# A planned fused kernel (complex linear attention and two MLPs): each kind of transfer, and the attention's matmuls, get a duration of their own in the planner

## The chip, the cores and the metric

The kernel runs on one core of a Trainium2 chip. The metric is device time in microseconds (us), lower is better. The profile is one execution of the whole program, taken by the hardware profiler; its times count from the start of its span.

## The reference, cut to what matters

Sizes: batch 4, 8 heads, 768 steps, head size 48; the MLPs are 384 wide with 2048 hidden units.

```python
scale = minimum(mag, 0.999) / (mag + 1e-6)        # mag = |a_re + i a_im|
for t in range(S):                                # complex decay, real k v, per head
    S_re, S_im = ar*S_re - ai*S_im + k_t v_t, ar*S_im + ai*S_re
    y[t] = q_t @ S_re
x = y as (4*768) rows of 384
h = x @ w_in1;  x = maximum(0.01*h, h) @ w_out1
h = x @ w_in2;  out = where(h > 0, h, exp(min(h, 0)) - 1) @ w_out2
```

## The kernel before

**Attention.** The recurrence is cut into chunks of 128 steps: 6 chunks times 4 batches give 24 tiles, `attention(0)` to `attention(23)`. ACT and DVE turn the decays of a tile into products of magnitudes and sums of angles. DVE writes scaled k and q into the tile `st` (L459, one product for the cosine half and one for the sine half). The two halves leave for a scratch in HBM (L466, `stack_scratch<-st`) and come back in another layout as `f` (L469, `f<-stack_scratch`): two transfers out, two transfers in. PE transposes `st` (L485), multiplies `f` by `f` into scores (L498), and DVE masks them into `am` (L503). PE multiplies scores and state by v (L513, or L536 and L541), and from tile 3 on the result goes through a second scratch (L550 out, L553 back as `y`) and is split into two halves of 16 bits, `xh` and `xl` (L347, L348). L569 (`kv`) and the DVE steps L578 and L581 bring the running state up to date. There is one buffer for `st` and one for `f`.

**MLPs.** A block is three tiles, 384 columns. Eight blocks pass the first MLP and eight the second, in the order of the list ORDER. Each block runs over 16 slices of the hidden units. For a slice, L598 is a group of 9 matmuls into `h` (weights and inputs are pairs of 16-bit halves, three products over three column groups); ACT and DVE make `g` of it and split it (L607 to L612, L347, L348); L633 is a group of 9 matmuls into `acc`. The weights arrive as 64-bit words in 64 pieces (`wr`, three buffers, L311 and L314), and five steps on DVE and ACT convert a piece (L333, L335, L338, L341, L342). At the end of the list ACT reads the decays and weights once more for checks of range.

**What sets the order.** Nothing runs where it is written. Each step is given to `plan.op` with its engine, a duration, and what it reads and writes. `schedule` is a list scheduler: it walks through time, starts on each engine the ready step of the best rank, and takes an engine as busy for the duration given. `order` runs it three times with ranks improved from a backward pass and keeps the plan that ends first. The instructions are then issued in the order of the planned starts, so each engine's queue is fixed before the chip sees it: an instruction that waits on the chip holds everything behind it on its engine. A transfer is two steps: the issue on SP (475 ns) and the transfer itself on one "DMA" engine of the plan, with 650 ns ahead of it and some 900 to 1070 ns behind. The duration of the transfer was its bytes over 360, in ns. Where the plan shows PE idle for over 700 ns, the gap is filled with small matmuls on a constant (L753, `h<-ident`), (gap - 300) / 220 of them, so that PE does not lose its clock.

```python
if eng == "SP":
    self.ops.append([eng, self.ISSUE, fn, deps, due])
    self.ops.append(["DMA", ns / self.RATE, None, {m}, due])     # RATE = 360.0
```

Of the kernel before, what the change touches and what calls it, by code (L numbers as in the profile page):

```python
# [21 lines left out]
B, H, S, D = 4, 8, 768, 48  # L22
P = 128
C = 128
NC = S // C
NT = NC * B
DM = H * D
# [1 line left out]
DFF = 2048  # L29
KF = DFF // P  # L30
CW = 2 * C + 1
TILE_BYTES = 4 * DM * C
LAG = 2
SIZES = [3] * 8
ORDER = [1, 1, 1, 2, 1, 2, 1, 2, 1, 2, 1, 2, 1, 2, 2, 2]
# [86 lines left out]
class Plan:  # L122
# [8 lines left out]
            ("DMA", "DVE"): 907.0, ("DMA", "ACT"): 908.0, ("DMA", "PE"): 1067.0, ("DMA", "POOL"): 983.0}  # L131
    SWITCH = 1300.0
    ISSUE = 475.0
    RATE = 360.0
    ROUNDS = 3
    LAST = 1e9

# [7 lines left out]
    def op(self, eng, ns, fn, r=(), w=(), table=None, due=None):  # L145
        if table is not None and table != self.table:
            self.table = table
            self.ops.append([eng, self.SWITCH, lambda: self.load(table), set(self.group), None])
            self.group = [len(self.ops) - 1]
        m = len(self.ops)  # L150
        n = m + 1 if eng == "SP" else m
        deps = set()
        for x in r:
            deps.update(x.writers)
        for x in w:
            deps.update(x.writers)
            deps.update(x.readers)
        for x in (*r, *w):
            root = x.root
            if root.before is not None and not x.writers:  # L160
                deps.update(root.before.users)
            if root.last is not None and not root.users:
                deps.update(root.last.users[:1])
            root.users.append(n)
        for x in r:
            x.readers.append(n)
        for x in w:
            x.writers.append(n)
        if table is not None:
            deps.add(self.group[0])  # L170
            self.group.append(n)
        deps.discard(n)
        due = self.due if due is None else due
        if eng == "SP":
            self.ops.append([eng, self.ISSUE, fn, deps, due])
            self.ops.append(["DMA", ns / self.RATE, None, {m}, due])
        else:
            self.ops.append([eng, ns, fn, deps, due])

# [52 lines left out]

EXTRA = 97.0
SCAN = 350.0
YNS = 130.0
WARM = 8000.0
WARM_GAP = 700.0

# [9 lines left out]
def tile_due(i):  # L248
    return None
# [11 lines left out]
def fast_path(ctx, tc, aa, kq, vt, w_in1, w_out1, w_in2, w_out2, st_dram, yt_dram, out):  # L261
    nc = tc.nc
# [20 lines left out]
    plan = Plan(lambda table: nc.scalar.preload_act_table_set(sets[table]))  # L283
# [21 lines left out]
    def load_w(which, part, k):  # L305
        src = w_src[which, part].bitcast(I32)
        raw = plan.buf(cp, [P, DM, 2], I32, "wr", WR_BUFS)

        def load():
            if part == "in":  # L310
                nc.sync.dma_start(raw.t.rearrange("p (j f) w -> p j (f w)", j=KJ),  # L311
                                  src[:, 2 * k * P:2 * (k + 1) * P].rearrange("(j p) f -> p j f", p=P))
            else:
                nc.sync.dma_start(raw.t.rearrange("p o w -> p (o w)"), src[k * P:(k + 1) * P, :])  # L314

        plan.op("SP", 2 * TILE_BYTES, load, w=[raw])
        return raw

    def check_w(which, part, k, raw):
# [48 lines left out]
    def check_later(i):  # L368
        c, b = divmod(i, B)
        ar, ai = plan.buf(cp, [P, KJ, C], F32, "re"), plan.buf(cp, [P, KJ, C], F32, "im", 2)  # L370
        m2, sq = plan.buf(cp, [P, KJ, C], F32, "t0"), plan.buf(cp, [P, KJ, C], F32, "t8")
        plan.op("SP", TILE_BYTES, lambda: nc.sync.dma_start(ar.t, aa[c, b, :, 0]), w=[ar])
        plan.op("SP", TILE_BYTES, lambda: nc.sync.dma_start(ai.t, aa[c, b, :, 1]), w=[ai])
        check_re(i, ar, sq)
        plan.op("ACT", act(DM), lambda: S_.activation(sq.t, ai.t, AF.Square), r=[ai], w=[sq])
        plan.op("ACT", act(DM), lambda: S_.activation(m2.t, ar.t, AF.Square), r=[ar], w=[m2])
        plan.op("DVE", dve(DM), lambda: V.tensor_tensor(m2.t, m2.t, sq.t, ALU.add), r=[sq], w=[m2])
        check_m2(i, m2, sq)

    def attention(i):  # L380
        c, b = divmod(i, B)
# [3 lines left out]

        N = KJ * C
        ar, ai = plan.buf(cp, [P, KJ, C], F32, "re"), plan.buf(cp, [P, KJ, C], F32, "im", 2)
        plan.op("SP", TILE_BYTES, lambda: nc.sync.dma_start(ar.t, aa[c, b, :, 0]), w=[ar])
        plan.op("SP", TILE_BYTES, lambda: nc.sync.dma_start(ai.t, aa[c, b, :, 1]), w=[ai])
        x = plan.buf(cp, [P, KJ, 2, C], F32, "kq", 3)  # L390
        re, im = (lambda: ar.t), (lambda: ai.t)
        m2, sq, yr, t = tmp(0), tmp(8), tmp(1), tmp(2)
# [13 lines left out]
        w = tmp(3)  # L406
# [7 lines left out]
        def scan_p():  # L414
# [11 lines left out]
        plan.op("DVE", dve(N), lambda: V.tensor_tensor(tp.t, pr.t[:, :, 1], yp.t, ALU.mult), r=[pr, yp], w=[tp])  # L426
        plan.op("DVE", dve(N), lambda: V.scalar_tensor_tensor(
            pr.t[:, :, 0], tp.t, 2.0, yp.t, ALU.subtract, ALU.mult, reverse0=True), r=[tp, yp], w=[pr])
        plan.op("SP", 2 * TILE_BYTES, lambda: nc.sync.dma_start(x.t, kq[c, b]), w=[x])
        plan.op("DVE", dve(2 * N), lambda: V.tensor_tensor(x.t, x.t, pr.t, ALU.mult), r=[pr], w=[x])  # L430
        yield
        th = tmp(7)
# [30 lines left out]
        scr = st_dram[i % 2]  # L463
        dr = plan.buf(None, None, None, "scr", 2)
        for cs in range(2):
            plan.op("SP", 4 * DM * CW, lambda cs=cs: nc.sync.dma_start(  # L466
                scr[cs].rearrange("(j p) w -> p j w", p=P), st.t[:, cs]),
                r=[st.part(("e", cs)), st.part(cs)], w=[dr.part(cs)])
            plan.op("SP", 4 * DM * CW, lambda cs=cs: nc.sync.dma_start(  # L469
                f.t[D * cs:D * (cs + 1)], scr[cs].rearrange("(h d) w -> d h w", d=D)), r=[dr.part(cs)],  # L470
                w=[f.part(cs)])
        fp = [f.part(0), f.part(1)]

        v = plan.buf(cp, [P, H, D], F32, "v")
        plan.op("SP", TILE_BYTES, lambda: nc.sync.dma_start(v.t, vt[c, b]), w=[v])
        last = c == NC - 1
        pa = lambda: plan.buf(ps_a, [P, 512], F32, "pa", 3)
        if not last:
# [13 lines left out]
        for g in range(2):  # L492
            pt = pa()

            def sc(g=g, pt=pt):
                for hh in range(4):
                    h = 4 * g + hh
                    T_.matmul(pt.t[:, hh * C:(hh + 1) * C], lhsT=f.t[:, h, 0:C], rhs=f.t[:, h, C:2 * C],  # L498
                              start=True, stop=True)

            plan.op("PE", 4 * 218, sc, r=fp, w=[pt], due=tile_due(i))
            m = plan.buf(cp, [P, 4, C], F32, "am", 2)
            plan.op("DVE", dve(512), lambda m=m, pt=pt: V.tensor_tensor(  # L503
                m.t, pt.t.rearrange("p (h t) -> p h t", h=4), mask.unsqueeze(1).to_broadcast([P, 4, C]), ALU.mult),
                r=[pt], w=[m])
            am.append(m)
# [20 lines left out]
        else:  # L527
# [19 lines left out]
                yt.t[:wide].rearrange("p g t -> p (g t)"), py.t[:wide], AF.Copy, scale=SX), r=[py], w=[yt])  # L547
            yd, ys = yt_dram[i % 2], plan.buf(None, None, None, "yscr", 2)
            for r in range(2):
                plan.op("SP", TILE_BYTES // 2, lambda r=r: nc.sync.dma_start(  # L550
                    yd.rearrange("(g r e) t -> r e g t", r=2, e=D)[r], yt.t[64 * r:64 * r + D]), r=[yt], w=[ys.part(r)])
            y = plan.buf(cp, [P, KJ, C], F32, "y")
            plan.op("SP", TILE_BYTES, lambda: nc.sync.dma_start(y.t, yd.rearrange("(j p) t -> p j t", p=P)),  # L553
                    r=[ys.part(0), ys.part(1)], w=[y])
            xsrc, xap = y, lambda: y.t
        k, q = place[i]
# [7 lines left out]
        if not last:  # L564
            pk = pa()

            def kv():
                for h in range(H):
                    T_.matmul(pk.t[:2 * D, h * D:(h + 1) * D], lhsT=kn.t[:, h].rearrange("p a d -> p (a d)"),  # L569
                              rhs=v.t[:, h, :], start=True, stop=True)  # L570

            plan.op("PE", 8 * 163, kv, r=[kn.part(0), kn.part(1), v], w=[pk], due=tile_due(i))
            pk3 = lambda: pk.t[:2 * D, :DM].rearrange("p (h e) -> p h e", h=H)
            pe = lambda: f.t[:, :, 2 * C:2 * C + 1].to_broadcast([2 * D, H, D])
            if c == 0:
                plan.op("ACT", act(N, True), lambda: S_.activation(state[b].t, pk3(), AF.Copy), r=[pk], w=[state[b]])
            else:
                plan.op("DVE", dve(N), lambda: V.tensor_tensor(state[b].t, pk3(), state[b].t, ALU.add),  # L578
                        r=[pk], w=[state[b]])
            if c % 2:  # L580
                plan.op("DVE", dve(N), lambda: V.tensor_tensor(state[b].t, state[b].t, pe(), ALU.mult),  # L581
                        r=fp, w=[state[b]])
# [34 lines left out]
    def block(which, k):  # L617
# [38 lines left out]
        for o in range(outs):  # L656
            c, b = divmod(blk[o], B)
            e = plan.buf(cp, [P, DM], F32, "o", 2)
            if o % 2:
                plan.op("DVE", dve(DM), lambda o=o, e=e: V.tensor_scalar(  # L660
                    e.t, acc[o].t[:, :DM], 1.0 / (SG * SW), None, ALU.mult), r=[acc[o]], w=[e])
            else:
                plan.op("ACT", act(DM, True), lambda o=o, e=e: S_.activation(
                    e.t, acc[o].t[:, :DM], AF.Copy, scale=1.0 / (SG * SW)), r=[acc[o]], w=[e])
            plan.op("SP", TILE_BYTES, lambda e=e, r0=b * S + c * C: nc.sync.dma_start(out[r0:r0 + C, :], e.t), r=[e])


    running = {i: attention(i) for i in range(NT)}
# [268 lines left out]
```

## Time and profile before

| | |
|---|---|
| runs | 1018.89, 1020.98, 1015.18 us; median 1018.89 |
| profiled execution, its own time | 1022.27 us |
| its span | 1020.6 us |
| PE busy (matmuls) | 942.7 us, 92% |
| PE weight loads | 628.7 us, 62% |
| ACT busy | 723.8 us, 71% |
| DVE busy | 688.3 us, 67% |
| POOL busy | 52.4 us, 5% |
| transfers of the SP queue | 127.97 MB, 45.2% of 16 engines' span |

PE is busy for nearly the whole span, but busy is not even over it: the first fifth holds most of its idle time, and there DVE, ACT and the transfers are dense too. From about 345 us to the end PE hardly stops. PE's clock is granted in full (2.4 GHz) or in half (1.2 GHz), and the half shows in short stretches behind idle ones. The matmuls on a constant count as busy PE.

### The profile page before, as it was taken

The numbers are of one execution on the slowest core, as the hardware profiler recorded it, in microseconds if no ns is written. First come the engines' busy times: TensorE is split into PE (matmuls) and PEld (weight loads), VectorE is DVE, ScalarE is ACT, GpSimd is POOL, SyncE is SP. The second block draws the span as 40 slices with busy tenths as digits, with TensorE's granted clock in tenths as the row PEclk, the third lists the DMA queues.
The fourth block names the chain that finished last, engine by engine and source line by source line (L and its number), as shares of the span: only waits on it lengthen the run. The fifth ranks groups of instructions, "written<-read, shape, count | busy, mean of one in ns | idle before, by whom it ended". The sixth has DMA issues, their size and how long they took to land.

```text
span 1020.6 us, 17938 instructions
## 1 busy us (share of the span) xinstructions
PE 942.7 (92%) x6486; PEld 628.7 (62%) x6486; DVE 688.3 (67%) x1450; ACT 723.8 (71%) x1686; POOL 52.4 (5%) x113
## 2 busy tenths in 40 slices
PE   4487988899999899999999989999999999999997
PEld 3486756556666665666666766575566666666664
DVE  7898887889998873685657777755644443544452
ACT  6576763668868763785568678899899998855552
POOL 4001300100000000000000000000000000000000
PEclk8699899999999999999999999999999999999999
DMA  6787966654556631440231565244746644000000
GB/s 227 197 226 190 254 145 169 168 155 115 157 170 182 182 80 39 122 127 17 70 94 55 138 158 162 85 111 147 210 155 167 191 153 135 32 1 24 2 24 27
DMA packets 110033, 129.20 MB, mean 127 GB/s; under 512 B 6768, under 2 KB 98672, under 8 KB 109936
## 3 DMA queue, kind: packets, MB, share of 16 engines
q1 hardware_dynamic: 109936, 127.97, 45.2%
q8 instruction: 53, 0.87, 0.4%
q14 instruction: 44, 0.36, 0.1%
HBM read 100.15 MB, written 27.80 MB: 125 GB/s over the span
## 4 chain that ended last, share of the span: by engine, by line
PE 59%; DMA 16%; ACT 11%; DVE 10%; issue 3%; POOL 1%; SPq 1%; ACTq 0%; DVEq 0%; POOLq 0%
PE acc L633 26%; PE h L598 25%; DMA f<-stack_scratch 6%; PE pa L498 3%; DMA stack_scratch<-st 3%; ACT t L324 2%; DMA turned_scratch<-am 2%; DMA y<-turned_scratch 2%; ACT gh L347 1%; PE pa L569 1%; PE pa L536 1%; DMA wr<-in_w_out 1%; DVE st L459 1%; ACT g L609 1%; PE pa L541 1%
## 5 line engine op out<-in xcount | busy, mean ns | idle before, releaser
L633 PE MATMUL acc<-gh,w1out 128*128 128x384 f16 x768 | 188.8, 328 | 4.0 <-DVE yl L650 2.4
L633 PE MATMUL acc<-w2out,gh 128*128 128x384 f16 x768 | 188.0, 327 | 0.2 <-DVE yl L650 0.2
L348 DVE TENSOR_TENSOR gl<-g,gh 128x384 f16<-128x384 f32 x256 | 141.2, 552 | 67.7 <-ACT gh L347 65.5
L612 DVE SCALAR_TENSOR_TENSOR g<-h,g 128x384 f32<-128x384 f32 x256 | 141.5, 553 | 54.7 <-ACT g L607 51.3
L347 ACT ACTIVATE gh<-g 128x384 f16<-128x384 f32 x256 | 132.5, 518 | 60.6 <-PE acc L633 56.4
L598 PEld LDWEIGHTS <-w1in 128*128 128x128 f16 x1152 | 113.6, 99 | 80.3 <-issue 8.5
L633 PEld LDWEIGHTS <-w1out 128*128 128x128 f16 x1152 | 113.0, 99 | 77.6 <-issue 7.5
L598 PEld LDWEIGHTS <-w2in 128*128 128x128 f16 x1152 | 112.3, 98 | 75.6 <-issue 2.7
L598 PE MATMUL h<-xh,w1in 128*128 128x384 f16 x768 | 148.2, 330 | 4.6 <-DVE g L612 4.4
L598 PE MATMUL h<-yh,w2in 128*128 128x384 f16 x768 | 145.8, 326 | 1.3 <-DVE g L612 1.3
L633 PE MATMUL acc<-gl,w1out 128*128 128x384 f16 x384 | 126.0, 328 | 0.0
L633 PE MATMUL acc<-w2out,gl 128*128 128x384 f16 x384 | 125.4, 326 | 0.0
L611 DVE TENSOR_SCALAR g<-g 128x384 f32<-128x384 f32 x128 | 45.7, 357 | 115.3 <-ACT g L610 115.1
L609 ACT ACTIVATE g<-h 128x384 f32<-128x384 f32 x128 | 62.1, 485 | 65.6 <-PE h L598 51.6
L633 PEld LDWEIGHTS <-gh 128*128 128x128 f16 x768 | 74.7, 98 | 48.6 <-issue 2.5
L607 ACT ACTIVATE g<-h 128x384 f32<-128x384 f32 x128 | 61.8, 483 | 49.6 <-PE h L598 31.7
L598 PE MATMUL h<-xl,w1in 128*128 128x384 f16 x384 | 84.4, 329 | 0.0
L598 PE MATMUL h<-yl,w2in 128*128 128x384 f16 x384 | 83.3, 326 | 0.0
L498 PE MATMUL pa<-f 96*128 96x128 f32 x384 | 56.4, 301 | 29.1 <-DMA f<-stack_scratch 25.6
L324 ACT ACTIVATE t<-wt,consts 128x384 f32<-128x384 f32 x128 | 78.0, 609 | 1.3
L498 PEld LDWEIGHTS pa<-f 96*128 96x128 f32 x384 | 52.7, 212 | 33.8 <-issue 23.5
L610 ACT ACTIVATE g<-g 128x384 f32<-128x384 f32 x128 | 66.5, 520 | 2.1
(111 smaller groups left out, 1259.4 us busy)
## 6 DMA issues: line engine op xcount, KB each, us to landing
wr<-in_w_in SPq DMA_DIRECT2D x64, 384.0 KB, 3.4
wr<-in_w_out SPq DMA_DIRECT2D x64, 384.0 KB, 3.4
stack_scratch<-st SPq DMA_DIRECT2D x48, 385.5 KB, 4.7
f<-stack_scratch SPq DMA_DIRECT2D x48, 385.5 KB, 5.8
kq<-in_kq SPq DMA_DIRECT2D x24, 384.0 KB, 5.0
re<-in_aa SPq DMA_DIRECT2D x32, 192.0 KB, 2.9
im<-in_aa SPq DMA_DIRECT2D x32, 192.0 KB, 3.0
v<-in_v SPq DMA_DIRECT2D x24, 192.0 KB, 3.1
```

What stands on the lines that cost most here:

```text
L324: plan.op("ACT", act(DM) + 2 * EXTRA, lambda side=side, scale=scale, bias=bias: S_.activation(z.t, t.t, AF.Relu, scale=scale, bias=bias, a ...
L347: plan.op("ACT", eng, lambda: S_.activation(hi(), v(), AF.Copy), r=r, w=wh)
L348: plan.op("DVE", dve(n), lambda: V.tensor_tensor(lo(), v(), hi(), ALU.subtract), r=r + wh, w=wl)
L459: plan.op("DVE", dve(2 * N), lambda cs=cs, tab=tab: V.tensor_tensor(st.t[:, cs, :, 0:2 * C].rearrange("p j (k t) -> p j k t", k=2), x.t, t ...
L498: T_.matmul(pt.t[:, hh * C:(hh + 1) * C], lhsT=f.t[:, h, 0:C], rhs=f.t[:, h, C:2 * C], start=True, stop=True)
L598: T_.matmul(ph.t[:, :n], lhsT=w.t[:, z, j * P:(j + 1) * P], rhs=x.t[:, j, :n], start=(m == 0), stop=(m == len(seq) - 1))
L607: plan.op("ACT", act(n, True), lambda: S_.activation(g.t[:, :n], ph.t[:, :n], AF.Copy, scale=0.01 * c), r=[ph], w=[g])
L609: plan.op("ACT", act(n, True), lambda: S_.activation(g.t[:, :n], ph.t[:, :n], AF.Relu, scale=-1.0 / (SX * SW)), r=[ph], w=[g])
L610: plan.op("ACT", act(n), lambda: S_.activation(g.t[:, :n], g.t[:, :n], AF.Exp, scale=-1.0), w=[g], table="L")
L611: plan.op("DVE", dve(n, True), lambda: V.tensor_scalar(g.t[:, :n], g.t[:, :n], -1.0, SG, ALU.add, ALU.mult), w=[g])
L612: plan.op("DVE", dve(n), lambda: V.scalar_tensor_tensor(g.t[:, :n], ph.t[:, :n], c, g.t[:, :n], ALU.mult, ALU.max), r=[ph], w=[g])
L633: T_.matmul(acc[o].t[:, :width], lhsT=pair[0], rhs=pair[1], start=(f == 0 and m == 0), stop=(f == KF - 1 and m == 2))
```

## The change

Only numbers given to the planner change. No instruction is added, removed or altered but the matmuls on a constant, whose number follows the plan. The transfer's duration is now the number itself, in ns, chosen by kind of transfer, and three numbers of the attention's matmuls move. (Old values are bytes over 360: 546 for 192 KB, 1092 for 384 KB.)

| step | planned before, ns | now, ns |
|---|---|---|
| decays `re`, `im`, `v`, output `o` | 546 | 480 |
| `kq` | 1092 | 960 |
| weights `wr`, first matrix / second matrix | 1092 | 1200 / 940 |
| `stack_scratch<-st`, each half | 1097 | 1800 |
| `f<-stack_scratch`, each half | 1097 | 2350 |
| `turned_scratch<-am` / `y<-turned_scratch` | 273 / 546 | 290 / 1000 |
| scores L498, group of four | 872 | 892 |
| scores and state by v (L536, L541), each | 130 | 119 |
| `kv` L569, eight | 1304 | 1320 |

```diff
-    RATE = 360.0
...
-            self.ops.append(["DMA", ns / self.RATE, None, {m}, due])
+            self.ops.append(["DMA", ns, None, {m}, due])
...
-YNS = 130.0
+YNS = 119.0
...
-            plan.op("SP", 4 * DM * CW, lambda cs=cs: nc.sync.dma_start(
+            plan.op("SP", 1800, lambda cs=cs: nc.sync.dma_start(
                 scr[cs].rearrange("(j p) w -> p j w", p=P), st.t[:, cs]),
...
-            plan.op("SP", 4 * DM * CW, lambda cs=cs: nc.sync.dma_start(
+            plan.op("SP", 2350, lambda cs=cs: nc.sync.dma_start(
                 f.t[D * cs:D * (cs + 1)], scr[cs].rearrange("(h d) w -> d h w", d=D)), r=[dr.part(cs)],
```

The order of the whole program shifts. Lines after the first constants stand two lines higher in the changed kernel (L498 is L496 there). Two places:

On PE, the scores of tile 3. `h<-ident` are the matmuls on a constant, `h<-xl` the last of a group of nine of the first MLP. Before:

```order
L598 LDWEIGHTS w1in_185
L598 MATMUL h<-xl,w1in_185 128x384
L753 MATMUL h<-ident 128x128 x8
L498 MATMUL pa<-f 128x128 x8
L753 MATMUL h<-ident 128x128 x4
L536 MATMUL pa<-am,v 64x128
```

Now:

```order
L596 LDWEIGHTS w1in_236
L596 MATMUL h<-xl,w1in_236 128x384
L496 MATMUL pa<-f 128x128 x8
L596 LDWEIGHTS w1in_277
L596 MATMUL h<-xh,w1in_277 128x384
```

One whole group (nine matmuls, of the third slice) has moved ahead of the scores, and one (the fourth) stands between the scores and their product with v, where matmuls on a constant stood.

On DVE, the twelve instructions that end with the first mask of tile 6 (`am`). Before:

```order
L342 SCALAR_TENSOR_TENSOR w1out11_1511<-wr_1162,w1out11_1511 128x384
L338 SCALAR_TENSOR_TENSOR wr_1406<-wr_1406,wt_1509 128x384
L333 TENSOR_SCALAR wt_1543<-wr_1453 128x384
L348 TENSOR_TENSOR gl_1550<-g_1451,gh_1538 128x384
L335 SCALAR_TENSOR_TENSOR wt_1543<-wr_1453,wt_1543 128x384
L342 SCALAR_TENSOR_TENSOR w1in12_1548<-wr_1406,w1in12_1548 128x384
L338 SCALAR_TENSOR_TENSOR wr_1453<-wr_1453,wt_1543 128x384
L612 SCALAR_TENSOR_TENSOR g_1535<-h_1477,g_1535 128x384
L410 TENSOR_SCALAR t3_1204<-t3_1204 128x384
L333 TENSOR_SCALAR wt_1579<-wr_1541 128x384
L342 SCALAR_TENSOR_TENSOR w1out12_1574<-wr_1453,w1out12_1574 128x384
L503 TENSOR_TENSOR am_1589<-pa_1568,mask_72 128x512
```

Now:

```order
L336 SCALAR_TENSOR_TENSOR wr_1543<-wr_1543,wt_1657 128x384
L346 TENSOR_TENSOR xl_1699<-y_1226,xh_1300 128x3x128
L331 TENSOR_SCALAR wt_1705<-wr_1601 128x384
L457 TENSOR_TENSOR st_1651<-kq_1008,t4_1664 128x3x256
L610 SCALAR_TENSOR_TENSOR g_1690<-h_1639,g_1690 128x384
L346 TENSOR_TENSOR gl_1723<-g_1603,gh_1624 128x384
L340 SCALAR_TENSOR_TENSOR w1in14_1707<-wr_1543,w1in14_1707 128x384
L346 TENSOR_TENSOR gl_1740<-g_1630,gh_1670 128x384
L610 SCALAR_TENSOR_TENSOR g_1738<-h_1672,g_1738 128x384
L457 TENSOR_TENSOR st_1651<-kq_1008,t5_1687 128x3x256
L331 TENSOR_SCALAR wt_1760<-wr_1697 128x384
L501 TENSOR_TENSOR am_1763<-pa_1743,mask_72 128x512
```

The mask of tile 6 now stands behind more work, the two `st` products of tile 7 among it: between the second `st` product of tile 6 and its first mask there were 22 instructions and are 34.

## Rows read from the trace of the kernel before

**Rows 1.** PE's waits over the whole span, the largest for data: total us, times, longest us.

```profile
PE pa L498 <- DMA f<-stack_scratch: 25.6, 9, 4.6
```

**Rows 2.** Stretches: us, busy (instructions) of PE, PEld, DVE, ACT, POOL, PEclk, DMA, GB/s.

```profile
92.00:215.00 123.00, 102.98 (x752) 74.56 (x751) 97.36 (x206) 71.93 (x155) 14.62 (x18) 0.93 0.73 188
...
345.00:1003.00 658.00, 647.16 (x4362) 410.42 (x4361) 385.67 (x792) 491.20 (x1181) 10.48 (x41) 1.00 0.36 100
```

**Rows 3.** PE in order of time, 92 to 215: start, us, [idle before <-releaser].

```profile
102.58 3.75 PE L498 MATMUL pa<-f 96*128 96x128 f32 x16 [4.56 <-DMA f<-stack_scratch]
...
131.84 3.25 PE L498 MATMUL pa<-f 96*128 96x128 f32 x16 [3.27 <-DMA f<-stack_scratch]
...
156.04 3.53 PE L498 MATMUL pa<-f 96*128 96x128 f32 x16 [4.24 <-DMA f<-stack_scratch]
...
186.29 1.39 PE L498 MATMUL pa<-f 96*128 96x128 f32 x8 [3.58 <-DMA f<-stack_scratch]
```

**Rows 4.** Stretches behind two of these idle times and one later, columns as in group 2.

```profile
101.60:108.50 6.90, 5.92 (x30) 5.73 (x32) 3.14 (x8) 2.78 (x5) 0.00 (x0) 0.51 0.97 265
132.40:135.90 3.50, 3.50 (x18) 2.94 (x17) 1.93 (x4) 0.60 (x2) 0.00 (x0) 0.51 0.02 5
...
340.60:344.10 3.50, 3.36 (x13) 2.57 (x14) 2.78 (x6) 2.15 (x7) 0.00 (x0) 0.51 0.47 140
```

**Rows 5.** DVE's waits from 92 to 215: total us, times, longest us.

```profile
DVE am L503 <- PE pa L498: 11.2, 8, 3.2
DVE wt L333 <- DMA wr<-in_w_in: 6.6, 2, 4.8
DVE st L459 <- POOL st L457: 2.1, 1, 2.1
```

**Rows 6.** The chain that ended last, around tile 6: start, us, what.

```profile
142.47 0.96 DVE st L459
...
143.45 5.61 DMA stack_scratch<-st
...
149.12 6.79 DMA f<-stack_scratch
```

**Rows 7.** DVE in order of time around tile 6.

```profile
143.81 0.54 DVE L335 SCALAR_TENSOR_TENSOR wt<-wr,wt 128x384 int32<-128x384 int32 x1
144.28 0.55 DVE L578 TENSOR_TENSOR state<-pa,state 96x384 f32<-96x384 f32 x1
...
156.63 0.36 DVE L333 TENSOR_SCALAR wt<-wr 128x384 int32<-128x384 int32 x1 [4.79 <-DMA wr<-in_w_in]
...
157.91 0.69 DVE L503 TENSOR_TENSOR am<-pa,mask 128x512 f32<-128x512 f32 x1 [0.45 <-PE pa L498]
```

**Rows 8.** DMA issues by line: count, KB each, median us from issue to landing.

```profile
stack_scratch<-st SPq DMA_DIRECT2D x48, 385.5 KB, 4.7
f<-stack_scratch SPq DMA_DIRECT2D x48, 385.5 KB, 5.8
```

**Rows 9.** PE's other waits on `f`, behind 215, in order of time.

```profile
340.74 2.05 PE L498 MATMUL pa<-f 96*128 96x128 f32 x8 [3.46 <-DMA f<-stack_scratch]
456.90 1.13 PE L498 MATMUL pa<-f 96*128 96x128 f32 x8 [1.78 <-DMA f<-stack_scratch]
608.29 1.13 PE L498 MATMUL pa<-f 96*128 96x128 f32 x8 [1.03 <-DMA f<-stack_scratch]
794.60 1.13 PE L498 MATMUL pa<-f 96*128 96x128 f32 x8 [0.67 <-DMA f<-stack_scratch]
```

**Rows 10.** DVE's groups from 92 to 215, by line: the weight pieces' first step.

```profile
L333 DVE TENSOR_SCALAR wt<-wr 128x384 int32<-128x384 int32 x18 | 6.3, 351 | 7.0 <-DMA wr<-in_w_in 6.6 <-DMA wr<-in_w_out 0.4
```

**Rows 11.** The matmuls on a constant (L753) from 92 to 215.

```profile
92.00:215.00 123.00, 8.27 (x58) 7.54 (x56) 0.93 0.73 188
```

**Rows 12.** One group of nine on PE, in order of time.

```profile
144.98 1.14 PE L598 MATMUL h<-xh,w1in 128*128 128x384 f16 x6
...
146.44 0.49 PE L485 MATMUL pa<-ident,st 128*128 128x128 f32 x3
```

More of the change, by code (lines that the diff above doesn't have):

```diff
@@ L31 @@
 CW = 2 * C + 1
-TILE_BYTES = 4 * DM * C
 LAG = 2
@@ L314, in load @@
                 nc.sync.dma_start(raw.t.rearrange("p o w -> p (o w)"), src[k * P:(k + 1) * P, :])
-        plan.op("SP", 2 * TILE_BYTES, load, w=[raw])
+        plan.op("SP", 1200 if part == "in" else 940, load, w=[raw])
         return raw
@@ L371, in check_later @@
         m2, sq = plan.buf(cp, [P, KJ, C], F32, "t0"), plan.buf(cp, [P, KJ, C], F32, "t8")
-        plan.op("SP", TILE_BYTES, lambda: nc.sync.dma_start(ar.t, aa[c, b, :, 0]), w=[ar])
-        plan.op("SP", TILE_BYTES, lambda: nc.sync.dma_start(ai.t, aa[c, b, :, 1]), w=[ai])
+        plan.op("SP", 480, lambda: nc.sync.dma_start(ar.t, aa[c, b, :, 0]), w=[ar])
+        plan.op("SP", 480, lambda: nc.sync.dma_start(ai.t, aa[c, b, :, 1]), w=[ai])
         check_re(i, ar, sq)
@@ L387, in attention @@
         ar, ai = plan.buf(cp, [P, KJ, C], F32, "re"), plan.buf(cp, [P, KJ, C], F32, "im", 2)
-        plan.op("SP", TILE_BYTES, lambda: nc.sync.dma_start(ar.t, aa[c, b, :, 0]), w=[ar])
-        plan.op("SP", TILE_BYTES, lambda: nc.sync.dma_start(ai.t, aa[c, b, :, 1]), w=[ai])
+        plan.op("SP", 480, lambda: nc.sync.dma_start(ar.t, aa[c, b, :, 0]), w=[ar])
+        plan.op("SP", 480, lambda: nc.sync.dma_start(ai.t, aa[c, b, :, 1]), w=[ai])
         x = plan.buf(cp, [P, KJ, 2, C], F32, "kq", 3)
@@ L428, in attention @@
             pr.t[:, :, 0], tp.t, 2.0, yp.t, ALU.subtract, ALU.mult, reverse0=True), r=[tp, yp], w=[pr])
-        plan.op("SP", 2 * TILE_BYTES, lambda: nc.sync.dma_start(x.t, kq[c, b]), w=[x])
+        plan.op("SP", 960, lambda: nc.sync.dma_start(x.t, kq[c, b]), w=[x])
         plan.op("DVE", dve(2 * N), lambda: V.tensor_tensor(x.t, x.t, pr.t, ALU.mult), r=[pr], w=[x])
@@ L474, in attention @@
         v = plan.buf(cp, [P, H, D], F32, "v")
-        plan.op("SP", TILE_BYTES, lambda: nc.sync.dma_start(v.t, vt[c, b]), w=[v])
+        plan.op("SP", 480, lambda: nc.sync.dma_start(v.t, vt[c, b]), w=[v])
         last = c == NC - 1
@@ L499, in sc @@
                               start=True, stop=True)
-            plan.op("PE", 4 * 218, sc, r=fp, w=[pt], due=tile_due(i))
+            plan.op("PE", 892, sc, r=fp, w=[pt], due=tile_due(i))
             m = plan.buf(cp, [P, 4, C], F32, "am", 2)
@@ L549, in attention @@
             for r in range(2):
-                plan.op("SP", TILE_BYTES // 2, lambda r=r: nc.sync.dma_start(
+                plan.op("SP", 290, lambda r=r: nc.sync.dma_start(
                     yd.rearrange("(g r e) t -> r e g t", r=2, e=D)[r], yt.t[64 * r:64 * r + D]), r=[yt], w=[ys.part(r)])
             y = plan.buf(cp, [P, KJ, C], F32, "y")
-            plan.op("SP", TILE_BYTES, lambda: nc.sync.dma_start(y.t, yd.rearrange("(j p) t -> p j t", p=P)),
+            plan.op("SP", 1000, lambda: nc.sync.dma_start(y.t, yd.rearrange("(j p) t -> p j t", p=P)),
                     r=[ys.part(0), ys.part(1)], w=[y])
@@ L570, in kv @@
                               rhs=v.t[:, h, :], start=True, stop=True)
-            plan.op("PE", 8 * 163, kv, r=[kn.part(0), kn.part(1), v], w=[pk], due=tile_due(i))
+            plan.op("PE", 8 * 165, kv, r=[kn.part(0), kn.part(1), v], w=[pk], due=tile_due(i))
             pk3 = lambda: pk.t[:2 * D, :DM].rearrange("p (h e) -> p h e", h=H)
@@ L664, in block @@
                     e.t, acc[o].t[:, :DM], AF.Copy, scale=1.0 / (SG * SW)), r=[acc[o]], w=[e])
-            plan.op("SP", TILE_BYTES, lambda e=e, r0=b * S + c * C: nc.sync.dma_start(out[r0:r0 + C, :], e.t), r=[e])
+            plan.op("SP", 480, lambda e=e, r0=b * S + c * C: nc.sync.dma_start(out[r0:r0 + C, :], e.t), r=[e])
     running = {i: attention(i) for i in range(NT)}
```

## The prediction

> **What bounds the kernel now.** I read PE's waits first, then a table by stretches, then both engines in order of time where they wait. From 345 to 1003 us PE is busy 647.2 of 658 us at full clock [rows 2], and no order of the same instructions can give back more than the 10.8 us between. What is lost lies ahead: from 92 us, when the first MLP group starts, to 215 us PE is idle for 20.0 us and for 8.3 us more it runs matmuls on a constant [rows 2, 11]. The reason has one name: PE waited nine times, 25.6 us in all, at the scores L498 for the transfer of `f` [rows 1]. Four of the nine, 15.65 us, lie between 92 and 215 [rows 3] (tiles 3, 5, 6, 7; tile 4 did not wait), four behind it, 6.94 us [rows 9]; one of some 3 us stands ahead of 92. Behind each of the four PE's clock was granted at half, 1.2 instead of 2.4 GHz (0.51), with PE busy 5.92 us behind the first and 3.50 behind the second; the third and fourth stretch are like the second [rows 4]. Half of 5.92 + 3 x 3.50, 8.2 us, is lost too. So PE could win at most 15.65 + 8.2 = 23.9 us from these four waits.
>
> DVE sets how much of that can be had. In the same stretch it is busy 97.4 of 123 us [rows 2], and PE's groups wait for weights and inputs that DVE makes. DVE's own idle time there is 25.6 us: 11.2 for the scores at the masks `am`, 6.6 for weight pieces, 2.1 at `st`, the rest small [rows 5]. The two engines hold each other: `st` leaves DVE, two transfers later PE makes scores, and DVE, in order, stands at the mask until then.
>
> **Why they wait.** Tile 6 shows it whole [rows 6]: `st` starts on DVE at 142.47, its second half lies in HBM 5.61 us after 143.45, the read of `f` takes 6.79 us from 149.12, the scores start at 156.04 [rows 3], the mask at 157.91 [rows 7]. That is 15.4 us from `st` to mask. The medians of all tiles are 4.7 and 5.8 us for the two legs [rows 8]. The old table planned 1.1 us for each half of either leg, the new one 1.8 and 2.35; with the two halves one behind the other and the lags that stand in the table, the pair of legs goes from about 7 to about 10 us in the plan, where 12.5 were measured (143.45 to 149.12 + 6.79). The planner therefore now puts more between.
>
> The Trainium skill, page "DMA: Bandwidth & Descriptors", section "Anatomy of one DMA", gives a software-generated transfer 2.0 us plus its bytes over 436 GB/s; an estimate from that page is 2.9 us for each leg. By it the old plan was long enough and the sum would be zero; the 5.61 and 6.79 us of [rows 6] speak against it for this pair, and nothing below uses it.
>
> **The change, part by part.** No instruction of the computation changes, so each engine's work is the same and only idle time, clock and fillers can move.
>
> *Early tiles.* Between the second `st` product and the first mask of a tile, the order has these counts of DVE instructions for tiles 3 to 7: before 18, 27, 30, 22, 19; now 31, 33, 41, 34, 32. DVE starts one of the common kind every 0.47 us (143.81 to 144.28 [rows 7]). 22 of them and the product (0.95) are 11.3 us, 4.1 short of the 15.4 us, and DVE stood still for 4.79 + 0.45 us there [rows 7]; 31 are 15.5 us, which is the 15.4 us almost to the digit, and 32 to 41 are more. So DVE's waits at the masks should fall from 11.2 to about 1. The 2.1 us at `st` came from the single buffer, when tile 4's product followed tile 3's transfer too closely; the new order puts more DVE work between these two (the distance was the smallest among the early tiles) and I count it as gone. Together -12.3. On PE the order has the fitting thing: a group of nine takes 1.46 us (144.98 to 146.44 [rows 12]), and ahead of the scores of tiles 3 to 6 there stand 1.0, 3.7, 7 and 8.7 more MLP groups than before, for tile 7 some 2; the fillers shrink there by 5 (five times two of the 58 instructions that took 8.27 us [rows 11], 1.4 us, inside idle time). PE's bound of 23.9 is not what I take, because PE can't run ahead of the weights: the lesser, DVE's 12.3, is the term. Its ends: 0, when DVE waits elsewhere for as long, and 18, when 6 of the remaining idle time go too.
>
> *Late waits.* Behind 215 the order is nearly the old one, but before the scores of tiles 11, 18 and 23 two more groups (2.9 us) stand behind the product that frees `f`, and three more (4.4) for tile 14 behind its state step. Against waits of 3.46, 1.03, 0.67 and 1.78 us [rows 9] that takes 2.9 + 1.0 + 0.7 + 1.8 = 6.4, and half of 3.36 us at half clock behind the first [rows 4] 1.7: 8.1. PE alone is the bound there, so this counts on the path. In seven late tiles one group fewer (1.46, for tile 12 two) stands between scores and the product with v; 2.9 us are left, as eight tiles had before. I take -6, ends 0 and -8.
>
> *New waits.* An order that differs from tile 1 on meets each queue anew: SP issues in order, and a weight piece behind a read of `f` waits for that read's turn (the 4.79 us of [rows 7] are such a piece, issued right behind tile 6's read). Such things cannot be read from an order. Nearest row: 6.6 us for weight pieces now [rows 5]; I add 3, ends 0 and 8. There are nine more fillers in all (178 for 169), and the surplus stands ahead of the first MLP group, where PE waits for its first tiles anyway: 0. The changed times of L498, L536, L541, L569 and of the short transfers move a step by some ns: 0.
>
> *Sum:* -12.3 - 6 + 3 = -15.3 us against the profiled execution's own 1022.3 gives 1007. That execution stood 3.4 above the median of its runs, so for the median 1018.9 - 15.3 = **1004 us**. With the ends of the early term alone 998 to 1016; all ends together 993 to 1021.
>
> **Rivals.** *The transfers stretch (1016).* Around tile 3's read the DMA engines were 0.97 busy at 265 GB/s [rows 4]; where more work is packed into the same time, reads of `f`, `st` and weights overlap more, and each leg grows by what was planned. Then the early term is -5, the late one -2, new waits +4: -3. For it: the share of 0.73 from 92 to 215 [rows 2] leaves little room. Against: the bytes are the same, and PE waited for tile 5's read with nearly nothing queued behind it (5 GB/s in the stretch that follows [rows 4]).
>
> *The change doesn't do what it says (1019).* The planner is a greedy list; better numbers don't have to give a better list, and the order behind 345 us is almost the same. Gains at some tiles and losses at others cancel. The page's short legs would end here as well.
>
> *Weights starve DVE (1025, slower).* Place: L333 on DVE. With the masks no longer holding it, DVE asks for the 18 pieces of the stretch [rows 10] sooner, while three buffers and one in-order queue bring them no faster. If five more of them wait 4.8 us like the longest [rows 5], that is +24 against -12.3 and -6: +5.7. It decides for slower once the wait for weights passes about 30 us (now 6.6). Against it: the new order spreads the conversions more evenly between tiles 3 and 7 instead of bunching them.
>
> **How the numbers follow.** Forecast 0.62, stretched transfers 0.15, no effect 0.10, starved weights 0.13. A measurement of this kernel tells 0.5%, 5.1 us, from no change. Faster by more than that (below 1013.8): the forecast and the lucky end of the second case, 0.66; within 0.5%: 0.20; slower: the last case and a little of the third, 0.14. The range 993 to 1020 leaves out starved weights and the forecast's lucky end, less than 2 in 10.
>
> **What would show it.** Right: PE's wait at the scores for `f` falls from 25.6 to under 10 us, DVE's wait at the masks between 92 and 215 from 11.2 to under 3, fewer stretches at half clock between 100 and 215 us (now four behind these waits), block 1 of the first MLP starts some 10 us sooner, and the late waits of [rows 9] are gone. Wrong: DVE's idle time stays near 25 us but names weight pieces (third rival) or still the scores, with legs longer than 4.7 and 5.8 us (first rival); or the early stretch is shorter and PE waits more behind 345 us, where it has 10.8 us idle now.

## The result, and the profile after

The changed kernel takes 980.04 us (median; 978.78 to 981.33) beside 1019.84 us (1015.18 to 1020.98) for the kernel before: a ratio of 0.9618, 95% interval 0.9585 to 0.9652, or 39.8 us. The forecast was 1004, its range 993 to 1020: the direction was right, the size too small by a factor of 2.6. The profiled spans are 1020.6 and 978.5 us, 42.1 us apart, which is 2.3 more than the medians: before's profiled execution (1022.27 us) lay above its median.

The head of the page of after:

```profile
span 978.5 us, 17979 instructions
...
PE 931.4 (95%) x6504; PEld 624.0 (64%) x6504; DVE 687.4 (70%) x1450; ACT 725.5 (74%) x1686; POOL 60.4 (6%) x113
```

DVE and ACT did the same work as before (688.3 and 723.8 us then). PE's busy time fell by 11.3 us, part of it clock given back; the rest of the gain is idle time. PE's waits for data over the whole span (total us, times, longest us), to be held against [rows 1]:

```profile
PE pa L496 <- DMA f<-stack_scratch: 3.9, 3, 2.5
PE h L751 <- DVE g L610: 3.9, 1, 3.9
PE h L596 <- DVE g L610: 1.6, 2, 0.8
```

The wait for `f` fell from 25.6 us to 3.9. To see where the rest came from, the program is cut at one and the same piece of DVE's work: the start of its 25th L612 (L610 in after), the step that finishes `g` of a slice, and the start of the 256th and last one. Columns as in [rows 2]; the kernel before, then after:

```profile
0.00:222.80 222.80, 167.88 (x1253) 136.01 (x1254) 183.64 (x396) 138.20 (x295) 34.41 (x57) 0.89 0.72 195
222.80:1004.90 782.10, 766.02 (x5182) 487.57 (x5181) 501.82 (x1051) 583.18 (x1387) 17.99 (x56) 1.00 0.39 109
```

```profile
0.00:203.40 203.40, 164.35 (x1282) 133.78 (x1283) 184.75 (x399) 142.10 (x302) 35.75 (x60) 0.91 0.81 212
203.40:962.80 759.40, 758.22 (x5170) 485.05 (x5168) 499.85 (x1047) 581.01 (x1382) 24.70 (x53) 1.00 0.41 112
```

The first part is 19.4 us shorter, with DVE busy for the same 184 us: its idle time went from 39.2 to 18.7 us. The second part is 22.7 us shorter: PE's idle time went from 16.1 to 1.2 us and its busy time fell by 7.8 (two stretches at half clock give 3.4 of that, twelve matmuls fewer some 2; the rest I can't name). What follows the last L612 took 15.7 us in both. So the gain lies in two nearly equal parts: 19.4 us where the prediction had 12.3 less 3 for new waits, and 22.7 us where it had 6.

The early tiles did what was forecast. PE in order of time; the scores of tiles 3 to 7, to be held against [rows 3]:

```profile
105.64 1.95 PE L496 MATMUL pa<-f 96*128 96x128 f32 x16
...
117.44 1.95 PE L496 MATMUL pa<-f 96*128 96x128 f32 x16
...
135.22 1.13 PE L496 MATMUL pa<-f 96*128 96x128 f32 x8 [0.60 <-DMA f<-stack_scratch]
...
158.16 2.02 PE L496 MATMUL pa<-f 96*128 96x128 f32 x16 [0.80 <-DMA f<-stack_scratch]
...
173.57 2.02 PE L496 MATMUL pa<-f 96*128 96x128 f32 x16
```

Four waits, 15.65 us in all, became two, 1.40 us in all, and sixteen matmuls take 2 us instead of 3.3 to 3.8: the granted clock in the stretches that start with these scores is 1.00, where it was half. Between 92 and 199 us one stretch at half clock shows still (0.50 from 99.9 to 105 us), behind PE's wait of 3.9 us for `g`. The transfers did not get shorter. The chain around tile 6 in after, beside [rows 6] (start, us, what):

```profile
140.99 1.82 DVE st L457 x2
...
143.34 6.40 DMA stack_scratch<-st
...
149.76 8.27 DMA f<-stack_scratch
...
158.16 2.02 PE pa L496 x16
```

The two legs took 6.40 and 8.27 us, where they had taken 5.61 and 6.79, and still DVE does not stand at the mask. It is at work on `st` of tile 7 and on weights until the scores are there:

```profile
157.47 0.95 DVE L457 TENSOR_TENSOR st<-kq,t 128x768 f32<-128x768 f32 x1
159.04 0.36 DVE L331 TENSOR_SCALAR wt<-wr 128x384 int32<-128x384 int32 x1 [0.62 <-DMA wr<-in_w_in]
159.33 0.69 DVE L501 TENSOR_TENSOR am<-pa,mask 128x512 f32<-128x512 f32 x1
```

In [rows 7] the same mask came behind 4.79 and 0.45 us of standing still.

### The profile page after: what moved, and what is told of

Read it like the earlier page. It is cut to its first block, busy times and chain, and to the rows that moved or that the text cites. A ratio compares the mean times of both kernels' runs of the same rounds, so it can differ in the third digit from the quotient of the medians.

```text
span 978.5 us, 17979 instructions
## 1 busy us (share of the span) xinstructions
PE 931.4 (95%) x6504; PEld 624.0 (64%) x6504; DVE 687.4 (70%) x1450; ACT 725.5 (74%) x1686; POOL 60.4 (6%) x113
## 4 chain that ended last, share of the span: by engine, by line
PE 76%; DVE 11%; DMA 7%; ACT 2%; issue 2%; POOL 1%; SPq 0%; DVEq 0%; POOLq 0%; ACTq 0%
PE acc L631 32%; PE h L596 32%; PE pa L496 4%; DMA f<-stack_scratch 2%; DMA stack_scratch<-st 2%; PE pa L567 2%; PE pa L534 2%; PE h L751 1%; PE pa L539 1%; DVE pr L414 1%; DMA wr<-in_w_in 1%; DVE st L457 1%; DVE gl L346 1%; DVE wt L333 1%; DVE g L610 1%
## 5 line engine op out<-in xcount | busy, mean ns | idle before, releaser
L610 DVE SCALAR_TENSOR_TENSOR g<-h,g 128x384 f32<-128x384 f32 x256 | 141.8, 554 | 50.3 <-ACT g L605 46.5
L496 PE MATMUL pa<-f 96*128 96x128 f32 x384 | 49.6, 277 | 4.8 <-DMA f<-stack_scratch 3.9
L751 PE MATMUL h<-ident 128*128 128x128 f32 x356 | 48.4, 300 | 5.4 <-DVE g L610 3.9
## 6 DMA issues: line engine op xcount, KB each, us to landing
stack_scratch<-st SPq DMA_DIRECT2D x48, 385.5 KB, 4.7
f<-stack_scratch SPq DMA_DIRECT2D x48, 385.5 KB, 6.5
```

The costliest lines, as they stand in the source:

```text
L610: plan.op("DVE", dve(n), lambda: V.scalar_tensor_tensor(g.t[:, :n], ph.t[:, :n], c, g.t[:, :n], ALU.mult, ALU.max), r=[ph], w=[g])
L751: T_.matmul(acc.t[:, 3 * P:], lhsT=ident, rhs=ident, start=True, stop=True)
```

## The experiments

Twelve kernels, in three groups that each ran on one chip beside the kernel before (its medians: 1018.24, 1017.11 and 1014.74 us). All are edits of the kernel before, but for `e2`, which edits the changed one. Numbers such as 1800 / 2350 are the planned ns of each half of the write of `st` and of the read of `f`. The theory of the prediction, A in the texts on record, is that the planned length of these two legs makes the gain, early by way of DVE's waits.

**Which numbers do it?** `e1_legs_only` changes the two legs alone:

```diff
-            plan.op("SP", 4 * DM * CW, ...            # write of st
+            plan.op("SP", 1800 * plan.RATE, ...
-            plan.op("SP", 4 * DM * CW, ...            # read of f
+            plan.op("SP", 2350 * plan.RATE, ...
```

> The kernel before with only the two legs of st and f planned at 1800 and 2350 ns; every other number is the old one. Theory A (the planned length of these two legs is the cause): nearly the whole gain, 980 to 990 us, PE's wait at the scores for f under 6 us in all (25.6 before, 3.9 in the changed kernel), and the late waits of 1 to 3.5 us gone. Theory B (any new table gives another list, and this list was lucky): a time with no relation to 980, anywhere from 1000 to 1030 us, with several waits of 3 us and more left.

`e2_all_but_legs` is the changed kernel with these two put back:

```diff
-            plan.op("SP", 1800, ...
+            plan.op("SP", 4 * DM * CW / 360.0, ...
-            plan.op("SP", 2350, ...
+            plan.op("SP", 4 * DM * CW / 360.0, ...
```

> The changed kernel with the two legs back at 1097 ns; all other new numbers stay (weights, decays, y, the attention's matmuls). Theory A: the waits come back, PE waits 20 us or more at the scores for f, 1012 to 1025 us. Theory B, or a theory that the other numbers carry the gain: under 1005 us.

Measured: e1 977.28 us, ratio 0.9569 (0.9524 to 0.9614); e2 1015.36 us, 0.9964 (0.9935 to 0.9994). The two legs are the whole gain; e1 even lies 3 us below the range expected. The dozen other numbers give 3 us by themselves (0.6 to 6.6 by the interval), and nothing on top of the legs that could be told: the full change and e1 agree within their intervals. PE's wait for `f` in e2 is 18.5 us, most of the 25.6 of [rows 1], though not the 20 that were expected:

```profile
PE pa L496 <- DMA f<-stack_scratch: 18.5, 8, 4.2
```

**Is it PE's clock, or DVE's pace?** `e3_fillers` leaves the order and puts 18 more matmuls on a constant ahead of the scores of tiles 3, 5, 6 and 7, where PE waits, so that its clock stays up:

```diff
+            if g == 0 and i in (3, 5, 6, 7):
+                held.append(len(plan.ops))
...
+    for n in held:
+        idle[n] = idle.get(n, 0) + 18
```

> The order of the kernel before, with 18 more small matmuls on a constant ahead of the scores of tiles 3, 5, 6 and 7, that is inside PE's four early waits for f (15.65 us in all), so that PE should keep its clock there. If PE's own lost clock (8.2 us in these stretches) is on the path, 1010 to 1014 us; if DVE sets the pace of this stretch, the scores and groups behind them run faster but PE waits for DVE soon after, and the time is within 3 us of the kernel before.

Measured: 1020.4 us, 1.0011 (0.998 to 1.0041). The stretch behind tile 3's scores, half clock in [rows 4], ran at full clock, and the scores of tile 6 stood where they had stood (156.04 in [rows 3]):

```profile
101.60:108.50 6.90, 6.79 (x71) 6.32 (x70) 4.39 (x9) 5.64 (x11) 0.00 (x0) 1.00 1.03 277
```

```profile
156.50 2.02 PE L500 MATMUL pa<-f 96*128 96x128 f32 x16 [1.68 <-DMA f<-stack_scratch]
```

Ahead of tile 7's scores DVE's product `kq`, which starts at 183.66 us in the kernel before, starts at 182.45:

```profile
182.45 0.96 DVE L432 TENSOR_TENSOR kq<-kq,pr 128x768 f32<-128x768 f32 x1
189.97 0.56 DVE L616 SCALAR_TENSOR_TENSOR g<-h,g 128x384 f32<-128x384 f32 x1 [6.57 <-PE h L759]
```

So the clock behind the scores of tiles 3, 5 and 6, half of 12.92 us [rows 4] or 6.5 us, is worth 1.2 us at most as long as DVE's waits stay. At tile 7 e3 is no clean test: the added matmuls write the tile that `h` lies in, DVE waited 6.57 us for it, and the lead was gone. The unchanged time of the whole program therefore speaks for tiles 3 to 6 only.

**Write or read? And would longer do better still?** One leg each, and both at 1.3 and 2 times the new numbers:

```diff
e5_read_only    1097 / 2350        e6_write_only   1800 / 1097
e7_legs_longer  2400 / 3100        e8_legs_double  3600 / 4700
```

> The kernel before with only the read of f planned longer (2350 ns, old 1097); the write of st stays at 1097. Theory A1 (what counts is that enough work stands between st and the scores, and the read carries most of the added length, 2 x 1.25 of the 2 x 1.95 us): most of the gain, 985 to 998 us. Theory A2 (half of the gain comes through the single st buffer, whose write the plan took for too short, so that DVE stops at the next tile's st and everything behind it): 998 to 1008 us, with DVE's waits at st (POOL L457 and stack_scratch, 14.6 us before) still above 8 us and PE's waits for DVE's g (5.7 before) still above 3.

> The kernel before with only the write of st planned longer (1800 ns, old 1097). A1: a small gain, 1005 to 1014 us, with PE's waits at the scores for f still 12 us or more. A2: DVE's waits at st fall below 8 us, PE's waits for g below 3, and the time is 996 to 1005 us.

> As the run with the legs only, but planned a third longer, 2400 and 3100 ns (the two halves then take some 13 us in the plan, about what is measured). If more distance is still better, 970 to 976 us. If the remaining waits (about 3 us at the scores) are all that is left to win and the plan now keeps PE idle for transfers that are done earlier (286 matmuls on a constant instead of 189, about 0.25 us each), 985 to 1005 us.

> As the run with the legs only, but planned twice as long, 3600 and 4700 ns, well over what is measured. The price of an overstated leg: the plan sees PE idle and issues 602 matmuls on a constant; if those stand on PE's path, some 80 to 110 us more than with the right length, 1050 to 1090 us; if they fall into time that PE waits for DVE anyway, under 1010 us.

Measured: read alone 985.11 us, 0.9686 (0.9666 to 0.9706); write alone 1006.09, 0.9905 (0.9879 to 0.9931). The two gains, 32.0 and 11.0 us, add up to about that of both together (41.0 in e1). The times are those of theory A1. A2, the single `st` buffer, failed in e6: DVE's waits at `st` are 10.9 us there (under 8 expected) and PE's for `g` 9.4 (under 3 expected; 5.7 before). Against A1, PE's wait for `f` in e6 is 9.8 us, not 12 or more. PE's waits for `g` between the 25th and the last L612, in e5 and in e6 (5.4 us before):

```profile
PE h L598 <- DVE g L612: 3.0, 3, 2.2
```

```profile
PE h L598 <- DVE g L612: 7.4, 7, 1.5
```

Longer: 1006.83, 0.9895 (0.9872 to 0.9919); double: 1093.01, 1.0751 (1.0725 to 1.0778); both some 2 to 3 us above the ranges expected. Of the lengths tried, e1's is the best. Two more points were taken later:

```diff
e12_legs_halfway  1450 / 1725        e11_legs_plus8  1950 / 2550
```

> As the run with the legs only, but halfway between the old and the new length, 1450 and 1725 ns. A gain that grows with the length planned: 992 to 1003 us, with DVE's idle time up to the 24th group between the 39.0 us of before and the 14.5 us of the run with the legs only.

> As the run with the legs only, but planned some 8% longer, 1950 and 2550 ns. If the time falls smoothly towards the measured length and rises behind it, 972 to 985 us; if a third more was already past a cliff of the list and not a slope, this one may lie anywhere between 977 and 1007.

Measured: halfway 996.99, 0.9819 (0.9756 to 0.9882); 8% longer 987.66, 0.9729 (0.9684 to 0.9774), which is worse than e1 by more than both intervals. Most of that shows early: e11 reaches the 25th L612 at 206.3 us, e1 at 197.2. Each length was tried with the one list that the planner makes of it, so whether the 8% costs this or the luck of a list does is not shown; that far too short and far too long are both worse is.

What an overlong leg costs shows in the matmuls on a constant, which stand for time that the plan believes PE to be idle. From 92 us on, those instructions alone in e1 (the order with 1800 / 2350) and in e7 (each counts as two records):

```profile
92.00:197.00 105.00, 6.46 (x52) 5.93 (x50) 1.00 0.86 222
```

```profile
92.00:216.00 124.00, 33.25 (x242) 31.68 (x242) 0.96 0.75 200
```

Over the whole span there are 602 of them in e8 and 169 before. In e8 the 25th L612 starts at 324.8 us, with DVE idle for 95.1 us until then. The likely reason is that the plan holds its DMA engine to be taken and puts MLP work late; what it takes for idle is then idle on the chip too, or filled, for the queues are fixed.

**Every transfer longer?** `e4_all_slower` plans all bytes at 170 instead of 360:

```diff
-    RATE = 360.0
+    RATE = 170.0
```

> The kernel before with one rate for all transfers, 170 instead of 360 bytes per ns: the legs are planned at 2322 ns each, as long as measured, but weights (2313), kq (2313) and decays (1157) twice as long as well. If it is enough that the legs are planned long, 978 to 992 us; if the kinds must differ, the one planned DMA engine is overfull in the first 200 us (it carries some 30 us of planned transfers more), weights come late in the plan and the time is 995 to 1015 us.

Measured: 1097.47 us, 1.0754 (1.0692 to 1.0816), far outside what either theory had. It has each half of the two legs at 2322, the read as in e1 and the write about as in e7, but also the weights and the rest at about twice their number, and it ends like e8: the 25th L612 starts at 320.0, DVE idle for 90.1 of it. Longer everywhere is not safer. All transfers share one DMA engine in the plan; which of the longer numbers does the harm was not tried.

**Are the two parts of the gain one?** The new legs for tiles 0 to 8 alone, and for tiles 9 to 23 alone:

```diff
+ e9_early_tiles:  1800 * plan.RATE if i < 9 else 4 * DM * CW        (2350 for the read)
+ e10_late_tiles:  1800 * plan.RATE if i >= 9 else 4 * DM * CW       (2350 for the read)
```

> The two legs planned at 1800 and 2350 ns for tiles 0 to 8 only, 1097 for tiles 9 to 23; all else old. If the early and the late gain are separate things (21 us up to the 24th group of nine of the first MLP, 21 us behind it, read from the two traces), this one has the early half: that group starts 18 to 26 us sooner than its 220.5 us before, and the time is 992 to 1001 us. If the late gain is only a consequence of the early one, 976 to 985 us.

> The two legs planned at 1800 and 2350 ns for tiles 9 to 23 only. Separate gains: the 24th group starts within 4 us of the kernel before and the time is 994 to 1004 us. A late gain that hangs on the early one: 1010 us or more.

Measured: early tiles 991.33, 0.977 (0.9719 to 0.9821); late tiles 1005.63, 0.9894 (0.986 to 0.9927), 1.6 us above its range. Each part comes without the other, so the late gain is no mere consequence of the early one; but 23.4 and 9.1 us add up to 32.5, not to the 41.0 of e1, and the rest is open. Until the 25th L612, e9 needs 197.6 us and e10 226.8 (before 222.8, e1 197.2). From there to the last L612, PE's waits for data in e9 and in e10:

```profile
PE h L598 <- DVE g L612: 7.4, 7, 1.6
PE pa L498 <- DMA f<-stack_scratch: 2.5, 3, 1.8
PE acc L633 <- DVE yl L650: 1.6, 3, 1.1
PE pa L498 <- ACT kn L488: 1.0, 1, 1.0
```

```profile
PE h L598 <- DVE g L612: 1.6, 3, 0.8
PE acc L633 <- DVE yl L650: 1.4, 2, 1.1
PE h L598 <- ACT xh L347: 1.2, 1, 1.2
```

That stretch is 775.1 us long in e9 and 763.0 in e10 (782.1 before). With the late legs planned longer, the waits for `f` and `kn` are gone, and most of those for `g`, although no step of the MLP has another number. Each of these stretches is from one execution: e10's span is 15.3 us shorter than before's, where the medians differ by 9.1.

## Why the prediction was right in kind and wrong in size

**Right: what bounds the kernel, and why.** The lost time lay behind the two legs, and their planned length decides it (e1, e2). DVE sets the early pace: its work until the 25th L612 is 183 to 185 us in before, after, e1, e5, e6 and e9, and what differs is its idle time; PE's clock alone is worth 1.2 us at most up to tile 6 (e3). So DVE's waits, not PE's, were the right ones to count for the early term.

**Wrong: the early part, -12.3 us and +3 for new waits, was -19.4, and DVE's idle time fell by 20.5.** The step that failed is the one that let DVE's other idle time stay. DVE's waits until the cut, before and after:

```profile
DVE am L503 <- PE pa L498: 12.6, 11, 3.2
DVE wt L333 <- DMA wr<-in_w_in: 11.8, 5, 4.8
DVE st L459 <- POOL st L457: 3.7, 2, 2.1
```

```profile
DVE wt L331 <- DMA wr<-in_w_in: 5.3, 6, 2.3
DVE am L501 <- PE pa L496: 4.0, 2, 3.6
...
DVE st L457 <- POOL st L455: 0.6, 2, 0.4
```

What I had counted came nearly as counted: the masks gave 8.6 us, less than the 10 of the sum (tile 3's first mask still waits 3.6 us, behind matmuls on a constant that wait for `g`, and the 4.0 us left miss the sign that I had named, under 3), and `st` 3.1, together 11.7 of 12.3. What I had left standing went as well: the weight pieces gave 6.5, for which I had added 3 instead, and the remaining 2.3 us are many small waits. The largest wait for a weight piece, the 4.79 us of [rows 7], was no price of its own: SP had issued the piece at 149.53 us, right behind the read of `f` at 148.31. In after DVE waits 0.62 us for a piece at this place. That an order which gives the read its time puts other work ahead of such a piece too is my reading of it, not tested by itself. My upper end for this term, 18, was too low as well; PE's bound of 23.9 held.

**New waits, +3.** One of this size came, though not for a weight piece: the 3.9 us that PE waits for `g` at a matmul on a constant, in the table of PE's waits above. DVE's 3.6 us at tile 3's mask stand behind it, so the early figure has it in it already. The top of my range is added up wrongly: with 0, 0 and 8 "all ends together" reach 1027, not 1021; the miss is at the other end.

**Wrong: the late term, -6 us, was -22.7.** I counted the late waits that bear the name `f` [rows 9]. They were 6.9 of the 15.9 us that PE waited in that stretch:

```profile
PE pa L498 <- DMA f<-stack_scratch: 6.9, 4, 3.5
PE h L598 <- DVE g L612: 5.4, 4, 2.2
PE pa L498 <- ACT kn L488: 1.8, 1, 1.8
PE acc L633 <- ACT o L663: 1.3, 1, 1.3
```

All of them go in after, where 1.0 us is left. The other 7.8 us of the 22.7 are PE's busy time, 3.4 of them at half clock; the 10.8 us of idle time between 345 and 1003, which I took for the most that could be had there, left such a gain out. Two of the four waits for `g`, 4.1 of the 5.4 us, came from the same two legs by a longer way. The trace of before shows it where PE stopped longest for `g`, in order of time (start, us, engine):

```profile
732.68 0.31 POOL L457 COPY st<-flags 128x3 f32<-128x3 f32 x2 [8.68 <-DMA stack_scratch<-st]
...
733.03 0.96 DVE L459 TENSOR_TENSOR st<-kq,t 128x768 f32<-128x768 f32 x1 [4.04 <-POOL st L457]
...
733.90 0.55 DVE L348 TENSOR_TENSOR gl<-g,gh 128x384 f16<-128x384 f32 x1
...
734.55 0.49 ACT L607 ACTIVATE g<-h 128x384 f32<-128x384 f32 x1 [3.53 <-DVE gl L348]
...
735.24 0.55 DVE L612 SCALAR_TENSOR_TENSOR g<-h,g 128x384 f32<-128x384 f32 x1
...
735.84 1.42 PE L598 MATMUL h<-xh,w1in 128*128 128x384 f16 x6 [2.24 <-DVE g L612]
```

The first row is the start of it: there is one buffer for `st`, a small copy into it on POOL had to wait until the write of the tile before had landed, and DVE stood 4.04 us for that copy. Behind it in DVE's queue stood `gl` and `g` of the MLP, ACT waited for the one and PE for the other, and PE's clock fell too (0.63 in the mean from 737 to 741 us). The wait that PE bears is called `g`; its cause is a transfer two engines away. The second such place has the same start and end:

```profile
602.11 2.02 DVE L459 TENSOR_TENSOR st<-kq,t 128x768 f32<-128x768 f32 x2 [2.38 <-DMA stack_scratch<-st]
...
605.64 1.14 PE L598 MATMUL h<-xh,w1in 128*128 128x384 f16 x6 [1.87 <-DVE g L612]
```

That the waits for `g` follow the planned legs is shown by e9 against e10 (7.4 and 1.6 us). That they follow DVE's standing at `st` is not: behind the cut DVE waits there 10.9 us before and still 8.1 in after, where PE waits 0.8 us for `g`. And it is the read's number that takes them away, not the write's: 3.0 us in e5 with the read alone planned longer, 7.4 in e6 with the write alone, where a late write to one buffer would have it the other way round. That speaks for a share of the order itself, in which PE needs what stands behind `st` less soon; how large it is, is not settled. A second buffer for `st`, which would tell it, was not tried.

A third way shows on ACT, which waits for `y`, the attention's result on its way through the other scratch. Before, e1, and e2:

```profile
ACT xh L347 <- DMA y<-turned_scratch: 17.8, 14, 3.2
```

```profile
ACT xh L347 <- DMA y<-turned_scratch: 1.5, 3, 0.8
```

```profile
ACT xh L345 <- DMA y<-turned_scratch: 13.7, 9, 3.6
```

The new number for `y` itself (1000 for 546) is in e2 and not in e1, so it isn't what takes most of these waits away, but the two legs, ahead of `y` in the same queue of transfers and in each tile's own chain. What these waits cost was not measured.

**The rivals.** The transfers did stretch: the read's median is 6.5 us where it was 5.8 [rows 8], and the DMA engines are busier over the early part (0.81 against 0.72). But at tile 6 it cost DVE no wait at the mask, because the new order had more work between than the legs needed; the rival had the fact right and its price wrong. Weights did not starve DVE: 13.2 us of waits for them became 6.6 until the cut. That a greedy list need not get better from better numbers is false for this change; beside e1 it is true for e7 and e11, whose planned legs are nearer to the measured ones and whose times are longer.

## What to carry to other kernels

When an order is fixed ahead by a planner, read the planned length of each transfer beside its length in the trace, correct the few that are far off and that others wait for, and measure on both sides: here the two legs at about three quarters of the best numbers tried lost 2.5% of the time again (ratio 0.982 against 0.957), at 1.3 times them 3.3%. When you price a wait that will go, don't take the waits that bear its name alone: follow each wait of the engine that bounds the stretch back through the queues in which its releaser stood, for a late transfer can be booked under whatever stood behind it. And before you add a price for new waits, ask whether the waits that you see now are its counterpart, and would go with their cause.

## What the runs showed of the hardware that I had not expected

The measured legs are far from a fixed time: 5.61 and 6.79 us for tile 6 before, 6.40 and 8.27 after, with the same 385.5 KB each and medians of 4.7 and 5.8, then 4.7 and 6.5 us. Yet the best planned numbers of those tried were neither these nor the highest: with 1800 / 2350 for each half the pair is planned at about 10 us, where 12.5 were measured, and 8% more on each was already worse. The best number for the plan need not be the one that the trace would put in. By the fit of the Trainium skill, page "DMA: Bandwidth & Descriptors", section "Anatomy of one DMA" (2.0 us plus the bytes over 436 GB/s, for transfers that GpSimd issues), 2.9 us a leg is an estimate. The legs here are issued by SP, and every one of these took longer.

The other thing is how little a full clock brings where PE isn't the bound: in e3 the granted clock behind the scores of tiles 3 and 5 rose from 0.51 to 1.00, and tile 6's scores started no sooner (156.50 us, 156.04 before).
